# A fused attention and gated MLP layer on one core: a closed head group leaves PSUM in one copy, DMAs move its sums and inverses, GpSimd multiplies and adds the residual, and VectorE's share of the softmax comes in batches of eight

## The chip, the core and the metric

The kernel runs on one core of a Trainium2 chip. The core has five engines with an instruction stream each: TensorE (PE, matmuls; PEld are its weight loads), VectorE (DVE), ScalarE (ACT), GpSimd (POOL) and SyncE (SP), which here only issues DMAs. SBUF is the core's working memory with 128 partitions; PSUM holds the results of matmuls in eight banks of 128 x 512 float32. The metric is the device time of one execution in microseconds (us).

## The reference

The input x is 2048 rows of 512 numbers in bfloat16. All of it is one layer:

```python
xn = _layernorm(x, axis=-1)
q = (xn @ wq) as 32 heads of 16;  k = xn @ wk;  v = xn @ wv      # one key/value head for all
p = softmax(einsum("bhqd,bkd->bhqk", q, k) * 16 ** -0.5)
s = einsum("bhqk,bkd->bhqd", p, v) as (2048, 512) @ wo
g = silu(silu(xn @ w1) @ w2)                                     # 512 -> 1792 -> 512
return x + s * g
```

There is no maximum subtracted and no mask. The 32 heads' scores of 2048 x 2048 (134 million exponentials) are most of the work outside TensorE.

## The kernel before, in words

**Tiles.** Queries are cut into four chunks of 512 (NC). Per chunk there are four "oi" of eight heads each, 16 in all, and each oi is closed in two head groups g = 2*oi + e of four heads. A group has 64 score tiles (SLOTS), each one bank: four 64x32-tile matmuls of `s_half` (L898) fill it with the scores of two heads against 64 keys (128 partitions) for 512 queries. In all there are 2,048 such tiles.

**Two ways to the exponential.** Either ACT takes the exponential of one or two neighbouring banks (`act_step`, L1605) into `pa_sb`; two value matmuls of `do_pv` (L1238) then add the tile to the group's output bank. Or DVE makes a first pass (`pass_d`, L974): it scales and offsets the score into a 16-bit integer whose bits are a bfloat16 near the exponential, in `db_sb`. Four tiles make a batch. POOL then adds three different constants to the whole batch (`split`, L1160, an `int64_add` on words of four numbers) into `ds_sb`, and the sum of the four versions, weighted through four copies of v, approximates the exponential. Such a tile takes eight value matmuls. A version of the shift on DVE (L1156) exists too, but is open only when many shifts wait or in the last group.

**Closing a group.** The value matmuls also carry a column of weights, so that row 16 of each block of 32 in the output bank holds the softmax's sum. When a group is complete, `make_norm` (L1247 to L1274) lets DVE transpose the bank in blocks of 32x32 in place (L1255), take the reciprocal of the sums (L1258), multiply into `otr_sb` (L1260), after which the bank is free, and for each pair of groups transpose back into `on_sb` (L1270). When the four oi of a chunk are in `on_sb`, a "w" job multiplies with wo (`mk_w`); `final` (L764) lets DVE multiply the result with the gate (L766) and add x (L769) into `ob_sb`, and SP stores it (L761). Loads of x for that sum are L777.

**Other work.** LayerNorm and its transposes stand in the first 60 us; "q", "h" and "z" jobs (L665) are the products with wq, w1 and w2, with a tanh on ACT (L713) and a product on DVE (L714) per result.

**Order.** A planner written in Python places every instruction when the kernel is built: it keeps a clock for each engine, charges each task a written duration (T_P 600 ns for a DVE pass, T_P64 for a shift, T_SH for a shift on DVE), and for each engine that is free picks the ready task of lowest priority number. A transfer is charged 60 ns on SP and is visible at issue + 1.4 us + size/(250 bytes per ns) + 0.6 us, the sizes one after the other. The order on each engine is then fixed; semaphore waits keep it right whatever the real durations. `s_step` decides for each free bank whether its tile goes to ACT or DVE by the backlogs of the two; `pick_d` opens a batch for DVE only while a group has at least MARGIN tiles left (MARGIN_END in the last group). Each engine runs its instructions in that order, so an instruction that waits holds all behind it. Tasks with `ports=2` on DVE and POOL are never placed side by side: each waits for the other's last one.

Of the kernel before, what the change touches and what calls it, by code (L numbers as in the profile page):

```python
# [15 lines left out]
P = 128  # L16
# [3 lines left out]
W1_AT, SKIP = 5, 1500.0  # L20
T_ISSUE, T_SWDGE = 450.0, 1000.0
J_BASE, J_END, MIXJ = 0.073, 1.084, 3
# [4 lines left out]
T_P, T_SH, T_TR, T_AF = 600.0, 600.0, 630.0, 63.5  # L27
T_P64, DV_MIN, T_LIB = 1015.0, 40, 300.0
HOLD_PO = 374.374
# [3 lines left out]
Q_URG = 0.308  # L33
J_SLIP = 1.308
NEXT_OB, OB_SLACK = 6, 192.595
NORM_PRIO, T_DIV = 0, 264.0
A_OPEN = 5
T_MS, V_AT = 500.0, 7
# [10 lines left out]
LINE, FETCH, FED, LOOK = 256, 3684.358, 58, 68  # L49
# [3 lines left out]
NPA, NDB, NDS, NTM = 21, 5, 8, 4  # L53
MARGIN, MARGIN_END = 19, 20
WIDE, PAIR_WAIT, GRP_WAIT = 14, 47.267, 237.034
Q_LEAD = 4.233
A_HIGH, D_HIGH, SLACK = 1582.599, 1518.392, 43.301
LEAD, CROWD, FRAG, DB_LOW = 468.141, 0.617, 2.417, 1
RUN, HOLD, PRESS = 6, 1411.229, 18
ROOM = 5  # L60
START_Z, START_H, AHEAD, NEAR = 8, 9, 1.03, 17
CLOSING, URGENT, END_DV = 2, 4.336, 55
STARVED = 511.14
JLATE, JEVAC = 1.311, 1
# [250 lines left out]
def bass_recurrent_scan__grouped_kv_mqa__dense_activation_silu__prompt_kernel(  # L315
# [29 lines left out]
    with ExitStack() as es:  # L345
# [3 lines left out]
        xn_sb = sb("xn_sb", [P, 4, D], BF16)  # L349
# [14 lines left out]
        db_sb = sb("db_sb", [P, NDB, 4 * NQ], U16)  # L364
        ds_sb = sb("ds_sb", [P, NDS, 4 * NQ], U16)
        f_sb = sb("f_sb", [P, 2, NQ], FP32)
        rcp_sb = sb("rcp_sb", [P, 2, NQ // 32], FP32)
        otr_sb = sb("otr_sb", [P, 2, NQ], BF16)
# [5 lines left out]
        ob_sb = sb("ob_sb", [P, 4, D], BF16)  # L374
# [12 lines left out]
        zer_sb = ob_sb[:, 3, :]  # L387
# [3 lines left out]
        XB = NDS - 4  # L391

        def x_tile(t):
            return ds_sb[:, XB + t // 4, (t % 4) * NQ:(t % 4 + 1) * NQ].bitcast(BF16)

# [17 lines left out]
        def xkey(t):  # L413
            return ("Ds", XB + t // 4, t % 4)

        def ds_keys(s):
            return [("Ds", s, h) for h in range(4)]
# [6 lines left out]
        for j in range(1, 4):  # L424
            dma(SP, "x", ds_sb[:, XB + j, :].bitcast(BF16).rearrange("p (t d) -> p t d", d=D),
                xv[:, 4 * j:4 * j + 4, :], 512, ds_keys(XB + j), prio=1)
# [15 lines left out]
        pl.add(Task(DV, 550.0, lambda v: v.memset(zer_sb, 0.0), (), [("ob", 3)], 0))  # L442
# [27 lines left out]
        for e in (1, 0):  # L470
# [16 lines left out]
        m1 = pl.add(Task(AC, 700.0, lambda a: a.activation(f_sb[:, 0, :], x_tile(1), ACT.Copy, scale=1.0 / D,  # L487
                                                          accum_out=mv_sb[:, 1, 0:1]),
                         [xkey(1)], [("F", 0), ("me", 1)], 0, gate=lambda: "scr2" in pl.lastw))
        m2 = pl.add(Task(AC, 210.0, lambda a: a.activation(scr_sb[:, 2:3], mv_sb[:, 1, 0:1], ACT.Copy, scale=-ISD),  # L490
                         [("me", 1)], ["nb"], 0, [m1]))
        pl.add(Task(AC, 700.0, lambda a: a.activation(f_sb[:, 0, :], x_tile(1), ACT.Square, scale=ISD, bias=scr_sb[:, 2:3],
                                                      accum_out=mv_sb[:, 1, 1:2]),
                    [xkey(1), "nb", ("me", 1)], [("F", 0), ("mv", 1)], 0, [m2]))
# [13 lines left out]
        for n in first:  # L508
# [18 lines left out]
            for i in tiles:  # L527
                xn_task[i] = pl.add(Task(DV, 323.0, lambda v, i=i: v.tensor_scalar(  # L528
                    xn_sb[:, i % 4, :], x_tile(i), mv_sb[:, i, 0:1], rstd_sb[:, i:i + 1],
                    op0=ALU.subtract, op1=ALU.mult),  # L530
                    [xkey(i), ("rs", a), ("mv", i)], [("xn", i % 4)], 1 + g, [t], ports=2,
                    gate=lambda i=i: i < 4 or i - 4 in t_done))
# [25 lines left out]
        def mk_T(tiles, bk=None):  # L558
            n, t0 = len(tiles), tiles[0]

            def rnd(b):
                def emit(pe, b=b):
                    dst = bank(b).bitcast(BF16).rearrange("p (t d) -> p t d", d=D)
                    h = None
                    for k, t in enumerate(tiles):
                        for dc in range(NDC):
                            h = pe.transpose(dst[:, k, dc * P:(dc + 1) * P], xn_sb[:, t % 4, dc * P:(dc + 1) * P], ident[:, :])
# [179 lines left out]
        def scaled(tt, b, r=None):  # L747
            k = tt % 2
            if r in EVR:
                ev = pl.add(Task(AC, 490.0, lambda a: a.activation(xn_sb[:, r, :], bank(b), ACT.Copy, scale=0.25),  # L750
                                 [("ps", b)], [("xn", r)], 0))
                fin_task[tt] = Task(DV, 333.0, lambda v: v.tensor_tensor(fin_sb[:, k, :], xn_sb[:, r, :], tmp_sb[:, tt % NTM, :], ALU.mult),
# [7 lines left out]
        def store(tt, t2):  # L760
            return pl.add(Task(SP, 60.0, lambda e: e.dma_start(of.rearrange("(t p) d -> p t d", p=P)[:, tt, :], ob_sb[:, tt % 4, :]),  # L761
                               [("ob", tt % 4)], [("out", tt)], 0, [t2], dma=128 * 1024, on_place=outs.append))

        def final(tt, b):  # L764
            k = tt % 2
            t1 = Task(DV, T_P, lambda v: v.scalar_tensor_tensor(  # L766
                out=bank(b), in0=bank(b), scalar=0.25, in1=tmp_sb[:, tt % NTM, :], op0=ALU.mult, op1=ALU.mult),
                [("ps", b), ("tmp", tt % NTM)], [("ps", b)], 0, [tmp_task[tt]])
            t2 = Task(DV, T_P, lambda v: v.tensor_tensor(ob_sb[:, tt % 4, :], bank(b), xr_sb[:, tt % 4, :], ALU.add),  # L769
                      [("ps", b), ("xr", tt % 4)], [("ob", tt % 4)], 0, [t1, xr_task[tt], out_task.get(tt - 4)])  # L770
# [5 lines left out]
        def add_xr(tt):  # L776
            xr_task[tt] = pl.add(Task(SP, 60.0, lambda e: e.dma_start(xr_sb[:, tt % 4, :], xv[:, tt, :]),  # L777
                                      (), [("xr", tt % 4)], 2, [fin_task[tt - 4]] if tt >= 4 else [], dma=128 * 1024))
# [3 lines left out]
        def mk_w(tt, pace):  # L782
            c, r = divmod(tt, 4)

            def consume(jb, op):
                t1, t2 = final(tt, jb.bank)
                if tt + 4 < NT:
                    add_xr(tt + 4)
                return [t1, t2]
# [151 lines left out]
        def pick_d(t):  # L941
            if st["assigned"] < 8 or any(k not in evac_kt or evac_kt[k].op is None for k in range(NKT)):
                return None
            for bt in batches:
                for k in range(4):
                    if k not in bt.slots and slot_time(bt.g, k % 2) <= t + 20:
                        return bt, k
            if any(len(bt.slots) < 4 for bt in batches):
                return None
            g = st["gD"]  # L950
            while g < NG and (nleft[g] < (MARGIN if g < NG - 1 else MARGIN_END) or min(len(left[g, i]) for i in range(2)) < 2):
# [7 lines left out]
            for k in range(2):  # L959
                if slot_time(g, k) <= t + 20:  # L960
                    bt = Job()
                    bt.g, bt.slots, bt.b, bt.P, bt.nsh, bt.left = g, {}, free[0], {}, 0, 4 * K
# [76 lines left out]
        def start_d(t, b, d):  # L1039
            bt, k = d  # L1040
            g, i = bt.g, k % 2
            if not bt.slots:
                batches.append(bt)
                db_busy[bt.b] = 1
                resv[g, 0], resv[g, 1] = 2, 2
# [63 lines left out]
        def make_shifts():  # L1109
            for bt in list(batches):  # L1110
                if len(bt.slots) < 4:
                    continue
                while bt.nsh < K - 1:
# [4 lines left out]
                    ds_busy[s] = 4  # L1118
# [594 lines left out]
```

## Time and profile before

| What | Value |
|---|---|
| time, median of 3 runs (lowest to highest) | 680.1 us (676.65 to 683.86) |
| time of the profiled execution | 674.7 us |
| its span, first to last instruction | 672.9 us |
| granted TensorE clock, mean | 1.000 |
| busy: PE / ACT / DVE / POOL | 660.8 / 653.9 / 632.6 / 612.1 us |
| score tiles through ACT / through DVE and POOL | 1,256 / 792 |
| HBM read, written | 8.95 MB, 2.10 MB |

A line of a group reads: source line, engine, operation, tile written <- tile read, shapes, count | busy us, mean ns of one | idle time of the engine just ahead of them and who ended it. Busy time counts a moment once even where two instructions of an engine overlap, so it is less than mean times count. A line of a wait reads: engine and line that waited <- engine and line that ended the wait: us in total, times, longest.

### The profile page before, as it was taken

To read this page: it belongs to the slowest core of one execution; us is meant where nothing else is said; L and a number is where in the kernel's file an instruction comes from. 1 tells how busy PE (TensorE), PEld (TensorE's weight loads), DVE (VectorE), ACT (ScalarE), POOL (GpSimd) and SP (SyncE) were. 2 spreads that over 40 slices of the span, in tenths; PEclk is the share of its full clock that TensorE was granted. 3 is DMA by queue.
4 is the path that set the end of the run, shared out by engine and by line. 5 is a ranking of instruction groups with operands and counts; after the bars stand their busy time and mean duration, and the time that the engine had idled before them with its cause. 6 is when DMAs were issued, how large, how long until landed. Compare 5 with 4: busy or idle time off the path is not lost.

```text
span 672.9 us, 47414 instructions
## 1 busy us (share of the span) xinstructions
PE 660.8 (98%) x22086; PEld 373.0 (55%) x22086; DVE 632.6 (94%) x1158; ACT 653.9 (97%) x1172; POOL 612.1 (91%) x610
## 2 busy tenths in 40 slices
PE   8999999999999999999999999999999999999996
PEld 4446656565555655555555656656656555556551
DVE  8989999999999999999999999999999999999932
ACT  6899999999999999999999999999999999999995
POOL 4049899999999999999999999999999999999990
PEclk9999999999999999999999999999999999999999
DMA  6412200000000000000000000000000001000000
GB/s 174 138 50 82 68 4 5 4 5 4 5 4 14 27 21 21 4 5 4 6 5 4 20 20 20 19 5 5 5 4 5 5 20 35 21 4 5 4 5 33
DMA packets 11782, 14.99 MB, mean 22 GB/s; under 512 B 1857, under 2 KB 10817, under 8 KB 11585
## 3 DMA queue, kind: packets, MB, share of 16 engines
q1 hardware_dynamic: 10976, 10.78, 5.4%
q8 instruction: 172, 2.82, 1.7%
q0 software_dynamic: 320, 0.92, 0.5%
q10 hardware_dynamic: 288, 0.26, 0.1%
q14 instruction: 26, 0.20, 0.1%
HBM read 8.95 MB, written 2.10 MB: 16 GB/s over the span
## 4 chain that ended last, share of the span: by engine, by line
PE 74%; ACT 20%; DVE 4%; POOL 1%; issue 0%
PE ps L898 31%; PE ps L1238 26%; ACT pa_sb L1605 19%; PE ps L665 16%; DVE stats_sb L499 1%; ACT t_sb L713 1%; DVE xn_sb L528 1%; POOL kt_sb L461 1%; PE ps L1446 0%; DVE kt_sb L611 0%; DVE xnT_sb L578 0%; DVE v_sb L639 0%; POOL v_sb L459 0%; DVE var_sb L522 0%; DVE var_sb L524 0%
## 5 line engine op out<-in xcount | busy, mean ns | idle before, releaser
L1605 ACT ACTIVATE pa_sb<-ps 128x512 bf16<-128x512 f32 (+1 forms) x1081 | 622.8, 759 | 6.9 <-PE ps L898 6.1
L1160 POOL INT64_ADD ds_sb<-db_sb x594 | 602.8, 1044 | 12.8 <-DVE db_sb L974 6.2
L898 PE MATMUL ps<-qt_sb,kt_sb 64*32 64x512 bf16 x8192 | 564.1, 379 | 0.8 <-issue 0.4
L974 DVE TENSOR_SCALAR db_sb<-ps 128x512 uint16<-128x512 f32 x792 | 493.2, 680 | 10.8 <-PE ps L898 5.9
L1238 PE MATMUL ps<-ds_sb,v_sb 64*32 64x512 bf16 x4752 | 413.6, 377 | 0.8 <-issue 0.6
L1238 PE MATMUL ps<-pa_sb,v_sb 64*32 64x512 bf16 x2512 | 330.7, 377 | 3.0 <-ACT pa_sb L1605 2.3
L898 PEld LDWEIGHTS ps<-qt_sb,kt_sb 64*32 64x32 bf16 x8192 | 197.6, 90 | 190.0 <-ACT pa_sb L1605 81.9
L1238 PE MATMUL ps<-db_sb,v_sb 64*32 64x512 bf16 x1584 | 191.6, 377 | 0.0
L1238 PEld LDWEIGHTS ps<-ds_sb,v_sb 64*32 64x32 bf16 x4752 | 166.7, 92 | 22.0 <-issue 3.4
L665 PE MATMUL ps<-w_sb,u_sb 64*32 64x512 bf16 x1792 | 140.1, 378 | 0.5 <-issue 0.5
L665 PE MATMUL ps<-xnT_sb,w_sb 64*32 64x512 bf16 x1792 | 136.3, 378 | 0.0
L1238 PEld LDWEIGHTS ps<-pa_sb,v_sb 64*32 64x32 bf16 x2512 | 101.6, 92 | 25.1 <-ACT pa_sb L1605 11.1
L1238 PEld LDWEIGHTS ps<-db_sb,v_sb 64*32 64x32 bf16 x1584 | 59.4, 92 | 5.9 <-issue 1.1
L665 PEld LDWEIGHTS ps<-w_sb,u_sb 64*32 64x32 bf16 x1792 | 48.8, 92 | 12.8 <-issue 2.6
L665 PEld LDWEIGHTS ps<-xnT_sb,w_sb 64*32 64x32 bf16 x1792 | 44.3, 91 | 16.4 <-DVE db_sb L974 2.2
L713 ACT ACTIVATE t_sb<-ps 128x512 bf16<-128x512 f32 x72 | 48.9, 679 | 0.0
L1255 DVE STREAM_TRANSPOSE ps<-ps 128x512 f32<-128x512 f32 (+1 forms) x33 | 23.3, 708 | 17.0 <-PE ps L1238 16.8
L714 DVE SCALAR_TENSOR_TENSOR u_sb<-t_sb,ps 128x512 bf16<-128x512 bf16 x56 | 37.9, 676 | 0.5 <-ACT t_sb L713 0.3
L665 PE MATMUL ps<-xnT_sb,wq_sb 64*32 64x512 bf16 x480 | 37.3, 378 | 0.0
L665 PE MATMUL ps<-wo_sb,on_sb 64*32 64x512 bf16 x384 | 29.6, 378 | 0.0
L1284 POOL DMA_DIRECT2D kt_sb<-kt_sb x4 | 2.8, 700 | 23.8 <-DVE kt_sb L611 14.6
L665 PEld LDWEIGHTS ps<-xnT_sb,wq_sb 64*32 64x32 bf16 x480 | 11.7, 91 | 4.1 <-DVE db_sb L974 0.7
(72 smaller groups left out, 181.8 us busy)
## 6 DMA issues: line engine op xcount, KB each, us to landing
xr_sb<-in_A_x_dram SPq DMA_DIRECT2D x16, 128.0 KB, 2.3
out_dram<-ob_sb SPq DMA_DIRECT2D x16, 128.0 KB, 1.7
w_sb<-in_B_w_dram SPq DMA_DIRECT2D x1, 1792.0 KB, 7.2
ds_sb<-in_A_x_dram SPq DMA_DIRECT2D x3, 512.0 KB, 7.0
w_sb<-in_B_w_dram SPq DMA_DIRECT2D x2, 512.0 KB, 4.3
kt_sb<-kt_sb POOLq DMA_DIRECT2D x4, 224.0 KB, 3.7
w_sb<-in_B_w_dram SPq DMA_DIRECT2D x2, 384.0 KB, 4.3
wq_sb<-in_A_wq_dram SPq DMA_DIRECT2D x1, 512.0 KB, 5.2
```

The lines of the kernel that those rows point to most:

```text
L461: pl.add(Task(PO, 3540.0, lambda g: g.memset(kt_sb[0:DH, 1, :, :], 0.0), [("xn", 3)], [("kt1", c) for c in range(NC)], 3, gate=lambda: all ...
L499: ts_ = pl.add(Task(DV, 593.0, lambda v, t=t: v.bn_stats(stats_sb[:, t, :], x_tile(t)), [xkey(t)], [("st", t)], 1 + j, gate=(lambda j=j: S ...
L528: xn_task[i] = pl.add(Task(DV, 323.0, lambda v, i=i: v.tensor_scalar(xn_sb[:, i % 4, :], x_tile(i), mv_sb[:, i, 0:1], rstd_sb[:, i:i + 1], ...
L665: h = pe.matmul(bank(b)[32 * j:32 * (j + 1), :], lhsT=lhs(k, rows, 32 * j, 32), rhs=rhs(k, rows), start=first, stop=last, tile_position=(r ...
L713: t1 = Task(AC, T_AF + 0.8333 * NQ, lambda a: a.activation(t_sb[:, k, :], bank(b), ACT.Tanh, scale=scale), [("ps", b)], [("t", k)], 0)
L714: t2 = Task(DV, T_P, lambda v: v.scalar_tensor_tensor(out=dst, in0=t_sb[:, k, :], scalar=1.0, in1=bank(b), op0=ALU.add, op1=ALU.mult), [(" ...
L898: h = pe.matmul(bank(b)[32 * j:32 * j + 32, :], lhsT=kt_sb[r0:r0 + 64, g % 2, i, k0:k0 + 32], rhs=qt_sb[r0:r0 + 64, g // 2 % NQR, :], star ...
L974: bt.P[k] = pl.add(Task(DV, T_P, lambda v: v.tensor_scalar(db_sb[:, bt.b, k * NQ:(k + 1) * NQ], bank(b), 128.0 * LOG2E, 128.0 * (SHIFT_BET ...
L1160: whole["po"].append(pl.add(Task(PO, T_P64, lambda g: g.int64_add(ds_sb[:, s, :].bitcast(U64), db_sb[:, bt.b, :].bitcast(U64), words), rea ...
L1238: h = pe.matmul(bank(OB)[q:q + 32, :], lhsT=lhs[rows], rhs=rhs[rows], start=s0, stop=s1, tile_position=(64 * l, q), skip_group_check=True)
L1255: t1 = pl.add(Task(DV, (T_TR - 60.0) / parts + 60.0, lambda v, cols=cols: v.transpose(bank(OB)[:, cols], bank(OB)[:, cols]), [("ps", OB)], ...
L1605: op = pl.place(AC, 0.8333 * NQ * n + T_AF, lambda a: a.activation(pa_sb[:, s * NQ:(s + n) * NQ].rearrange("p (b n) -> p b n", n=NQ), ps3[ ...
```

## The change

For the first 15 of the 16 oi, the groups close in another way (`moved_norm`). DVE copies the output bank to SBUF in float32 (`o_sb` for the even group, `e_sb` for the odd one), and the bank is free. DMAs on SP's queue gather the rows of sums of each group into `den_sb` as 128 x 16 numbers; DVE takes one reciprocal for both groups; two DMAs write the inverses to a scratch tensor in DRAM, one DMA fills `rr_sb` from it with each inverse repeated over the 16 rows of its head, four DMAs move the odd group's results to their partitions in `o_sb`; then POOL multiplies `o_sb` with `rr_sb` into `on_sb`. The last oi closes as before. In `final` for all but the last chunk, DVE writes its product to `fin_sb` and POOL adds x in place in `xr_sb`, which is stored from there; `ob_sb` is gone and other small tiles share memory.

Batches have eight tiles in place of four (BS = 8), so each shift is one `int64_add` over 4,096 numbers per partition; `db_sb` has 3 such buffers (5 of four before), `ds_sb` 4 (8 of four), `pa_sb` 24 tiles (21). The planner's written durations and its thresholds have other values, so the order of the whole program and the share of tiles for each engine are planned anew.

```diff
-T_P, T_SH, T_TR, T_AF = 600.0, 600.0, 630.0, 63.5
-T_P64, DV_MIN, T_LIB = 1015.0, 40, 300.0
+T_P, T_SH, T_TR, T_AF = 600.0, 1130.0, 630.0, 63.5
+T_P64, DV_MIN, T_LIB = 1812.0, 40, 300.0
...
+FIN_PRIO, ON_PRIO = 6.803, 3
+T_DMA, T_GT, T_REC = 3200.0, 1300.0, 252.0
...
-NPA, NDB, NDS, NTM = 21, 5, 8, 4
-MARGIN, MARGIN_END = 19, 20
+BS = 8
+NPA, NDB, NDS, NTM = 24, 3, 4, 4
+MARGIN, MARGIN_END = 26, 27
...
-A_HIGH, D_HIGH, SLACK = 1582.599, 1518.392, 43.301
+A_HIGH, D_HIGH, SLACK = 1370.087, 863.23, 45.072
...
-        db_sb = sb("db_sb", [P, NDB, 4 * NQ], U16)
-        ds_sb = sb("ds_sb", [P, NDS, 4 * NQ], U16)
+        db_sb = sb("db_sb", [P, NDB, BS * NQ], U16)
+        ds_sb = sb("ds_sb", [P, NDS, BS * NQ], U16)
...
-        def final(tt, b):
+        def final(tt, b, po=False):
             k = tt % 2
+            if po:
+                t1 = Task(DV, T_P, lambda v: v.scalar_tensor_tensor(
+                    out=fin_sb[:, k, :], in0=bank(b), scalar=0.25, in1=tmp_sb[:, tt % NTM, :], op0=ALU.mult, op1=ALU.mult),
+                    [("ps", b), ("tmp", tt % NTM)], [("fin", k)], 0, [tmp_task[tt], out_task.get(tt - 2)])
+                t2 = Task(PO, T_GT, lambda g: g.tensor_tensor(xr_sb[:, tt % 4, :], fin_sb[:, k, :], xr_sb[:, tt % 4, :], ALU.add),
+                          [("fin", k), ("xr", tt % 4)], [("xr", tt % 4)], FIN_PRIO, [t1, xr_task[tt]], ports=2)
+                fin_task[tt], out_task[tt] = t1, store(tt, t2)
+                pl.add(t2)
+                return [t1]
...
-                for k in range(4):
+                for k in range(BS):
...
-                    bt.g, bt.slots, bt.b, bt.P, bt.nsh, bt.left = g, {}, free[0], {}, 0, 4 * K
+                    bt.g, bt.slots, bt.b, bt.P, bt.nsh, bt.left = g, {}, free[0], {}, 0, BS * K
...
-                if len(bt.slots) < 4:
+                if len(bt.slots) < BS:
...
+        def shift_dma(name, size, out_, in_, reads, writes, preds, prio=-1):
+            task = pl.add(Task(SP, 60.0, lambda e: e.dma_start(out_, in_), reads, writes, prio, preds, dma=size * 1024))
+            task.ring = name
+            return task
+
+        def moved_norm(g):
+            oi, e = divmod(g, 2)
+            OB, k = ob[g], oi % 2
+            okeys = [("xn", 2 * k), ("xn", 2 * k + 1)]
+            dst, keys = (e_sb[:, :], ["eb"]) if e else (o_sb[:, k, :], okeys)
+            ev = norm[g] = pl.add(Task(DV, T_P, lambda v: v.tensor_copy(dst, bank(OB)), [("ps", OB)], keys, NORM_PRIO,
+                                       on_place=lambda op: pool_free.append(OB)))
+            nb = NQ // 32
+            norm["d", g] = shift_dma("den%d" % e, 300, den_sb[:, e, :], dst[DH:P:32], keys, [("den", e)], [ev])
+            if e == 0:
+                return
+            rec = pl.add(Task(DV, T_REC, lambda v: v.reciprocal(inv_sb[:, :, :], den_sb[:, :, :]), [("den", 0), ("den", 1)], ["inv"], 3,
+                              [norm["d", g - 1], norm["d", g]]))
+            put = [shift_dma("put%d" % q, 32, o_sb[32 * q + DH:32 * q + 2 * DH, k, :], e_sb[32 * q:32 * q + DH, :], ["eb", ("den", 0)] + okeys,
+                             [("moved", k, q)], [ev, norm["d", g - 1]]) for q in range(4)]
+            rows = [shift_dma("row%d" % a, 200, in_dram(a * NQ, [[2 * NQ, 4], [16, 32], [1, 16]]), inv_sb[:, a, :], ["inv"], [("row", a)], [rec])
+                    for a in range(2)]
+            fill = shift_dma("fill", 256, rr_sb[:, :], in_dram(0, [[NQ, 8], [0, DH], [1, NQ]]), [("row", 0), ("row", 1)], ["rr"], rows)
+            cc = oi // NOC - NON // NOC
+            t2_task[oi] = pl.add(Task(PO, T_GT, lambda p: p.tensor_tensor(on_sb[:, oi % NON, :], o_sb[:, k, :], rr_sb[:, :], ALU.mult),
+                                      okeys + ["rr"] + [("moved", k, q) for q in range(4)], [("on", oi % NON)], ON_PRIO, put + [fill], ports=2,
+                                      gate=lambda: cc < 0 or all(tt in w_rounds for tt in range(4 * cc, 4 * cc + 4))))
+
         def make_norm(g):
             oi, e = divmod(g, 2)
+            if oi < NO - 1:
+                return moved_norm(g)
```

## The prediction

> **What bounds the kernel now.** I read the page's first parts, then the busy time in windows, the waits, the costliest groups, and last the transfers.
>
> ```profile
> span 672.9 us, 47414 instructions
> PE 660.8 (98%) x22086; PEld 373.0 (55%) x22086; DVE 632.6 (94%) x1158; ACT 653.9 (97%) x1172; POOL 612.1 (91%) x610
> ```
>
> Four engines stand above 90%, so the average names no bound. The windows do (columns: window; then PE, PEld, DVE, ACT, POOL busy us, with instruction counts; clock; DMA share; GB/s):
>
> ```profile
> 25.00:125.00 100.00, 98.10 (x3172) 57.96 (x3176) 95.61 (x176) 96.81 (x177) 79.19 (x79) 1.00 0.14 38
> 225.00:325.00 100.00, 99.99 (x3492) 54.77 (x3484) 99.07 (x171) 99.90 (x185) 99.00 (x98) 1.00 0.04 13
> 325.00:425.00 100.00, 99.92 (x3476) 56.61 (x3468) 97.36 (x168) 99.90 (x179) 100.00 (x100) 1.00 0.06 15
> 650.00:673.00 23.00, 16.45 (x374) 6.06 (x351) 4.71 (x13) 15.67 (x20) 5.96 (x6) 1.00 0.08 25
> ```
>
> In the middle ACT, DVE and POOL are all full, and the clock is full throughout. PE's 99.9% is overlap of pipelined matmuls. From 125 to 625 us it does 17,338 matmuls, 34.7 a us; where the timeline shows it unhindered (near 343 us), a set of four on each of two lanes follows every 0.216 us, 37.0 a us. So PE runs at 94% of its own pace, and the waits name who holds it: mainly ACT, then DVE.
>
> ```profile
> PEld ps L898 <- ACT pa_sb L1605: 81.9, 336, 0.8
> PEld ps L898 <- DVE db_sb L974: 30.4, 136, 0.5
> POOL ds_sb L1160 <- DVE db_sb L974: 6.2, 4, 3.5
> ```
>
> The bound is therefore the joint throughput of ACT, DVE and POOL, which share the 2,048 score tiles: ACT takes the exponential of a tile (L1605), or DVE makes a first pass (L974) and POOL three shifts per batch of four (L1160). Work taken from one is worth something only if tiles are moved until all three are full again.
>
> ```profile
> L1160 POOL INT64_ADD ds_sb<-db_sb x594 | 602.8, 1044 | 12.8 <-DVE db_sb L974 6.2 <-PE ps L1238 4.8 <-PE ps L898 1.6
> L974 DVE TENSOR_SCALAR db_sb<-ps 128x512 uint16<-128x512 f32 x792 | 493.2, 680 | 10.8 <-PE ps L898 5.9 <-POOL ds_sb L1160 2.0 <-PE ps L1238 1.0
> L1255 DVE STREAM_TRANSPOSE ps<-ps 128x512 f32<-128x512 f32 x31 | 22.5, 725 | 3.4 <-PE ps L1238 3.2
> L1260 DVE TENSOR_TENSOR otr_sb<-ps,rcp_sb 128x256 bf16<-128x256 f32 x31 | 12.7, 411 | 0.1
> L1270 DVE STREAM_TRANSPOSE on_sb<-otr_sb 128x512 bf16<-128x512 bf16 x15 | 10.5, 703 | 0.0
> L769 DVE TENSOR_TENSOR ob_sb<-ps,xr_sb 128x512 bf16<-128x512 f32 x13 | 8.8, 678 | 0.0
> L1258 DVE RECIPROCAL rcp_sb<-ps 128x16 f32<-128x16 f32 x31 | 7.5, 240 | 0.1
> L456 POOL INT64_ADD lib_sb<-lib_sb x1 | 0.2, 230 | 0.1
> ```
>
> The reader is to see busy time and mean apart: instructions of one engine overlap at their ends, so the cost of one is busy over count. ACT: 622.8 over 1,256 tiles (906 single, 175 double) = 0.496 us a tile. DVE pass: 493.2/792 = 0.623. Shift: 602.8/594 = 1.015.
>
> **The change, part by part.** *DVE.* Thirty of 32 groups lose transpose, reciprocal and product: 30 x (0.725+0.240+0.411) = 41.3 us. Fifteen pairs lose the second transpose: 15 x 0.703 = 10.5. Added are 30 copies out of PSUM; the nearest row of that shape is L974, so 0.623 to 0.68, taken 0.65: 19.5. Fifteen reciprocals of 2x16: 16 numbers took 0.240, 8 took 0.189, so 32 are estimated at 0.34: 5.1. Twelve residual adds go: 12 x 0.678 = 8.1. Net -35.3 us. The first product of the output keeps its price with another destination.
>
> *POOL, shifts.* One word costs 0.230, 2,048 16-bit numbers per partition (512 words) 1.015, so the slope is 0.785 per four slots and eight cost 1.80 instead of 2.03. Same tiles: 297 x 1.80 = 534.6, that is -68.2. If the start cost is not shared the saving is nothing; that is the other end. Both points come from this operation, so I take 1.80.
>
> *POOL, new elementwise work:* 15 products and 12 adds of 128x512. No row shows a two-input operation on POOL. Below stands the memset of 128x512 (L459, 0.524), above twice the shift (2.09). The product reads 4 KB per partition, as much as the four-slot shift does in 1.04, so 1.2 is taken: 27 x 1.2 = 32.4 (14 to 56). POOL net: -35.8.
>
> [...]
>
> *The new balance.* Let s tiles move from ACT to DVE and POOL. With each engine's idle time kept, the span by ACT is 672.9 - 0.496s, by DVE 637.6 + 0.623s, by POOL 637.1 + 0.675s (three shifts of 1.80 over eight). ACT and POOL meet at s = 35.8/1.171 = 30.6: 657.7 us; DVE is then at 656.7. With s = 0 nothing is gained: ACT stays at 672.9.
>
> *PE.* A moved tile needs eight value matmuls instead of two: 184 more, 5 us at 37.0. PE's pace becomes 34.7 x 1.0085 x 623/608 = 35.9 a us, 97% of its own. That is cover enough, but thin. The closed bank is freed after one copy, 0.7 us, where around 328.8 to 331.1 us it took 2.3; this helps PE to a bank 30 times, and I set the two against each other at zero (each some 2 us).
>
> *Start and end.* POOL's first shift (43.8 us) waits for eight passes instead of four: 2.5 us of POOL, worth 2.5 x 0.496/1.171 = 1.1. At the end DVE's last pass starts at 643.5 and ACT works on alone until 662; a last batch must now open with 27 tiles left, not 20: up to 7 x 0.496 = 3.5, taken 1.7. Buffers hardly change (20 to 24 and 32 to 32 slots).
>
> *Transfers.* Nine DMAs per pair, 135 in all, on SP's queue, which otherwise stands waiting (L761 waits 468.8 us for DVE). An issue there takes 0.34 to 0.51 us, so 58 us of SP, hidden. Queued behind a store that waits for POOL's add are the next group's transfers. The chain sums -> reciprocal -> DRAM -> fill -> product is needed only by the output product some 25 us later, but DVE's reciprocal and POOL's product stand in in-order streams: behind the one are the passes, behind the other the shifts. The written plan gives the chain 3.2 + 0.25 + 3.6 + 3.05 = 10.1 us. The nearest rows:
>
> ```profile
> xr_sb<-in_A_x_dram SPq DMA_DIRECT2D x16, 128.0 KB, 2.3
> kt_sb<-kt_sb POOLq DMA_DIRECT2D x4, 224.0 KB, 3.7
> wk_sb<-in_A_wk_dram SPq DMA_DIRECT2D x1, 16.0 KB, 3.0
> wv_sb<-in_A_wv_dram SPq DMA_DIRECT2D x1, 16.0 KB, 4.2
> ```
>
> Small pieces land in 3.0, or 4.2 behind another. Chain: 3.0 + 0.34 + 0.4 + 3.0 + 3.0 to 3.7 = 9.7 to 10.4, so at most 0.3 us late, which POOL's shift in progress (half of 1.8) covers. I take nothing; with 4.2 for each leg it is 4.2+0.34+0.4+4.2+4.2 = 13.3, 3.2 us late.
>
> Sum: 672.9 - 15.2 + 1.1 + 1.7 = 660.5 span. The profiled execution took 674.7, 1.8 above its span, so 662.3. The median of the runs, 680.1, is 0.8% above that execution: 662.3 x 680.1/674.7 = 667.6, forecast **667 us**.
>
> **The rivals.** *No change.* POOL's two-input operations cost 2.09: POOL gains 68.2 - 56.4 = 11.8, s = 10, the balance 668 and with start and end 670.8, or 678 on the scale of the runs. PE's pace at 97% of its own with eight banks would do the same: its 6% of lost time may not shrink. For it: 81.9 us of waits on ACT. Against: those waits go when ACT is given fewer tiles. That the plan cannot move tiles in steps of eight ends here too, at 675 to 680.
>
> *Slower: late transfers stall full engines.* Each us by which the chain is later than planned stands on POOL (and its first leg on DVE), 15 times, and delays the shifts that PE is to consume. At 3.2 us: 15 x 3.2 = 48 lost, 667 + 48 = 715; at 2 us 697. It decides from 13/15 = 0.9 us per pair, where the gain is gone. For it: the legs are serial and the 4.2 row. Against: that row was taken while 0.66 of the DMA time was in use, and in the middle it is 0.02 to 0.06. [...]
>
> *More than forecast.* POOL's operations at 0.52 and less idle time on DVE (10 us in the middle): 650 to 658.
>
> **How the numbers follow.** Forecast 0.50 (660 to 673), more 0.12, no change 0.16, slower 0.22. Three runs lie within 1% of each other, so about 1% is what can be told from no change. Faster 0.62, same 0.16, slower 0.22. The range leaves out half of the slower case beyond 2 us of lateness and a little below: 650 to 697.
>
> **What would show it.** Passes L974's successor near 822, shifts near 308 at 1.80 us busy; exponential tiles near 1,226; POOL's two-input operations near 1.2; ACT, DVE and POOL full in the middle. Wrong if POOL or DVE show idle time released by a DMA, if shifts cost over 1.9, or if PE waits stay at 110 us while ACT and DVE are no longer full.

## The result, and the profile after

The changed kernel takes 1010.0 us (median, 1006.9 to 1014.88) against 680.29 for the kernel before: a ratio of 1.484 (95% interval 1.477 to 1.491), so 48% slower where 2% faster was forecast. The profiled execution took 1014.88 us, its span is 1013.0, 340.1 more than the 672.9 of before.

The page of the changed kernel, its first part, the granted clock in 40 slices and the shares of the chain that ended last by engine:

```profile
span 1013.0 us, 47350 instructions
PE 720.7 (71%) x22134; PEld 366.2 (36%) x22134; DVE 623.0 (62%) x1096; ACT 663.0 (65%) x1147; POOL 600.0 (59%) x341
PEclk9999897979797797977979869668979797787989
issue 33%; POOL 32%; PE 26%; DVE 4%; ACT 3%; DMA 0%; SPq 0%; POOLq 0%; DVEq 0%
```

The last two of these in the kernel before:

```profile
PEclk9999999999999999999999999999999999999999
PE 74%; ACT 20%; DVE 4%; POOL 1%; issue 0%
```

No engine is near full any more. DVE and POOL do less work than before, ACT 9 us more, and PE's 60 us more come with a lower granted clock (a mean of 0.853, 1.000 before); what has grown is idle time. A third of the chain that ended last is "issue", time in which an engine waited for nothing that the profile shows. The clock, 9 in every slice before, now falls in most of them. The middle, in the same columns as in the prediction:

```profile
225.00:325.00 100.00, 75.43 (x2420) 39.49 (x2408) 67.53 (x111) 71.02 (x124) 62.58 (x35) 0.86 0.06 15
325.00:425.00 100.00, 59.31 (x1772) 29.06 (x1772) 49.74 (x81) 52.41 (x87) 55.92 (x31) 0.81 0.04 12
```

Which engine stops first is told by the waits of the changed kernel (who waited for whom, us in total, times, longest) and by its groups of instructions (busy us, mean ns of one, idle time before them with its releasers):

```profile
ACT pa_sb L1659 <- PE ps L922: 298.7, 94, 13.8
DVE db_sb L998 <- POOL ds_sb L1184: 291.1, 33, 15.6
PEld ps L922 <- DVE db_sb L998: 173.7, 242, 13.8
...
POOL ds_sb L1184 <- issue: 148.4, 25, 6.4
...
POOL on_sb L1295 <- issue: 106.8, 15, 7.7
POOL xr_sb L785 <- issue: 70.8, 10, 7.5
```

```profile
L1184 POOL INT64_ADD ds_sb<-db_sb x298 | 558.2, 1889 | 192.2 <-issue 148.4 <-PE ps L1262 17.3 <-DVE db_sb L998 13.2
L1295 POOL TENSOR_TENSOR on_sb<-o_sb,rr_sb 128x512 bf16<-128x512 f32 x15 | 18.9, 1257 | 106.8 <-issue 106.8
L785 POOL TENSOR_TENSOR xr_sb<-fin_sb,xr_sb 128x512 bf16<-128x512 bf16 x12 | 13.6, 1140 | 70.8 <-issue 70.8
```

ACT waits for PE, PE for DVE, DVE for POOL's shifts, and POOL for nothing that the waits show. The products and adds themselves are short (1.26 and 1.14 us), but 7.1 us of silence stand ahead of one (106.8/15, 70.8/10) and 5.9 us ahead of the shift that follows (148.4/25). Only 10 of the 12 adds have it: two came right behind another product or add. So POOL leaves its shifts and comes back 25 times; each such trip is called an excursion below. 148.4 + 106.8 + 70.8 = 326.0 us, 96% of the 340.1 that the span grew. In the timeline of POOL in the changed kernel (start, us, instructions merged, idle before) it looks like this:

```profile
104.11 37.40 POOL L1184 INT64_ADD ds_sb<-db_sb  x20 [5.79 <-issue]
148.67 1.25 POOL L1295 TENSOR_TENSOR on_sb<-o_sb,rr_sb 128x512 bf16<-128x512 f32 x1 [7.16 <-issue]
156.05 35.53 POOL L1184 INT64_ADD ds_sb<-db_sb  x19 [6.13 <-issue]
```

The list of POOL's instructions in the built program shows what stands there. Before, an instruction without operands came once, ahead of the first `int64_add`. Now one stands wherever the kind changes between `int64_add` and `tensor_tensor` (rows 13, 15 and 17). There are 51 in the changed program, two for each excursion and the first:

```
12 L1184 ISA ds_sb<-db_sb 128x2048 x19
13 L1295 ISA
14 L1295 TensorTensor on_sb<-o_sb,rr_sb 128x512
15 L1184 ISA
16 L1184 ISA ds_sb<-db_sb 128x2048 x20
17 L1295 ISA
18 L1295 TensorTensor on_sb<-o_sb,rr_sb 128x512
```

The trace has it too, under the name MODIFY_POOL_CONFIG, in the views of a single source line (POOLq is POOL's sequencer; times, ns at least, in the middle and at most, first and last start in us). Three lines of the changed kernel, and the one of the kernel before:

```profile
L1295 POOLq MODIFY_POOL_CONFIG  x30: 1/8/16, 89.9 to 969.9; - x30
L785 POOLq MODIFY_POOL_CONFIG  x20: 1/1/33, 289.9 to 892.5; - x20
L1184 POOLq MODIFY_POOL_CONFIG  x50: 1/1/1, 98.5 to 978.3; - x50
L456 POOLq MODIFY_POOL_CONFIG  x2: 11/11/11, 0.9 to 0.9; - x2
```

There are two at each change. They take some nanoseconds; the silence lies behind them, 7.1 us up to the product or add and 5.7 of the 5.9 us up to the shift (in the middle of 25 each).

One such stop in windows of 2 us (columns as above), around the add at 297.03:

```profile
294.00:296.00 2.00, 2.00 (x82) 1.13 (x72) 1.75 (x3) 2.00 (x5) 0.00 (x0) 1.00 0.03 8
296.00:298.00 2.00, 0.68 (x28) 0.11 (x8) 0.00 (x0) 2.00 (x5) 0.97 (x1) 1.00 0.00 0
298.00:300.00 2.00, 0.00 (x0) 0.00 (x0) 0.00 (x0) 0.18 (x1) 0.17 (x1) 0.97 0.21 68
300.00:302.00 2.00, 0.00 (x0) 0.00 (x0) 0.00 (x0) 0.00 (x0) 0.00 (x0) 0.50 0.30 71
...
310.00:312.00 2.00, 2.00 (x48) 0.83 (x40) 1.22 (x2) 0.63 (x2) 2.00 (x2) 0.50 0.03 8
312.00:314.00 2.00, 2.00 (x56) 0.86 (x44) 1.38 (x2) 1.26 (x3) 1.56 (x1) 0.62 0.00 0
```

POOL falls silent near 290; the three buffers of passes cover some 6 us, then DVE, PE and ACT stop within 3 us of each other. About 3.2 us after PE stopped (at 296.7) the clock falls to 0.50, and it is back only some 5 us after PE has resumed (at 308.7): 48 matmuls in 2 us from 310, 82 in 2 us from 294. Over the 25 stops of PE in this trace the fall came 2.3 to 5.3 us after the stop (3.7 in the middle), and the clock was back 2.6 to 10.0 us after PE had resumed (4.5).

### The profile page after: what moved, and what is told of

Same layout as the page of the kernel before. It is cut to its first block, busy times and chain, and to the rows that moved or that the text cites. A ratio compares the mean times of both kernels' runs of the same rounds, so it can differ in the third digit from the quotient of the medians.

```text
span 1013.0 us, 47350 instructions
## 1 busy us (share of the span) xinstructions
PE 720.7 (71%) x22134; PEld 366.2 (36%) x22134; DVE 623.0 (62%) x1096; ACT 663.0 (65%) x1147; POOL 600.0 (59%) x341
## 4 chain that ended last, share of the span: by engine, by line
issue 33%; POOL 32%; PE 26%; DVE 4%; ACT 3%; DMA 0%; SPq 0%; POOLq 0%; DVEq 0%
POOL ds_sb L1184 28%; PE ps L922 11%; PE ps L1262 9%; PE ps L680 5%; ACT pa_sb L1659 3%; POOL on_sb L1295 2%; DVE db_sb L998 1%; POOL xr_sb L785 1%; DVE stats_sb L514 1%; DVE o_sb L543 0%; DMA o_sb<-e_sb 0%; POOL kt_sb L476 0%; PE ps L1500 0%; SPq L1272 0%; DVE kt_sb L626 0%
## 5 line engine op out<-in xcount | busy, mean ns | idle before, releaser
L998 DVE TENSOR_SCALAR db_sb<-ps 128x512 uint16<-128x512 f32 x800 | 504.0, 684 | 353.7 <-POOL ds_sb L1184 291.1
L922 PE MATMUL ps<-qt_sb,kt_sb 64*32 64x512 bf16 x8192 | 605.8, 402 | 109.1 <-DVE db_sb L998 107.1
L1184 POOL INT64_ADD ds_sb<-db_sb x298 | 558.2, 1889 | 192.2 <-issue 148.4
L1262 PE MATMUL ps<-ds_sb,v_sb 64*32 64x512 bf16 x4800 | 396.9, 406 | 72.4 <-POOL ds_sb L1184 70.7
L1262 PE MATMUL ps<-pa_sb,v_sb 64*32 64x512 bf16 x2496 | 264.5, 394 | 31.0 <-POOL ds_sb L1184 29.8
L1262 PE MATMUL ps<-db_sb,v_sb 64*32 64x512 bf16 x1600 | 167.8, 398 | 46.7 <-POOL ds_sb L1184 46.7
L1262 PEld LDWEIGHTS ps<-ds_sb,v_sb 64*32 64x32 bf16 x4800 | 141.3, 97 | 113.8 <-POOL ds_sb L1184 75.7
L1262 PEld LDWEIGHTS ps<-pa_sb,v_sb 64*32 64x32 bf16 x2496 | 81.1, 95 | 57.0 <-POOL ds_sb L1184 33.7
L1295 POOL TENSOR_TENSOR on_sb<-o_sb,rr_sb 128x512 bf16<-128x512 f32 x15 | 18.9, 1257 | 106.8 <-issue 106.8
L785 POOL TENSOR_TENSOR xr_sb<-fin_sb,xr_sb 128x512 bf16<-128x512 bf16 x12 | 13.6, 1140 | 70.8 <-issue 70.8
```

The source lines that it names most:

```text
L785: t2 = Task(PO, T_GT, lambda g: g.tensor_tensor(xr_sb[:, tt % 4, :], fin_sb[:, k, :], xr_sb[:, tt % 4, :], ALU.add), [("fin", k), ("xr", t ...
L922: h = pe.matmul(bank(b)[32 * j:32 * j + 32, :], lhsT=kt_sb[r0:r0 + 64, g % 2, i, k0:k0 + 32], rhs=qt_sb[r0:r0 + 64, g // 2 % NQR, :], star ...
L998: bt.P[k] = pl.add(Task(DV, T_P, lambda v: v.tensor_scalar(db_sb[:, bt.b, k * NQ:(k + 1) * NQ], bank(b), 128.0 * LOG2E, 128.0 * (SHIFT_BET ...
L1184: whole["po"].append(pl.add(Task(PO, T_P64, lambda g: g.int64_add(ds_sb[:, s, :].bitcast(U64), db_sb[:, bt.b, :].bitcast(U64), words), rea ...
L1262: h = pe.matmul(bank(OB)[q:q + 32, :], lhsT=lhs[rows], rhs=rhs[rows], start=s0, stop=s1, tile_position=(64 * l, q), skip_group_check=True)
L1295: t2_task[oi] = pl.add(Task(PO, T_GT, lambda p: p.tensor_tensor(on_sb[:, oi % NON, :], o_sb[:, k, :], rr_sb[:, :], ALU.mult), okeys + ["rr ...
```

## The experiments

The theories, by the letters that the expectations use. S: each change of kind on POOL, to a two-input operation and back, costs its two stops, whatever stands between. L, the slower rival of the prediction: late transfers stall POOL and DVE. B: with batches of eight and few buffers POOL waits for its neighbours, which takes the gain of the longer shift. M: the added transfers disturb the other streams. Ratios are to the kernel before on the same chip.

### One kind of instruction on POOL

The kernel called e1 below: the 27 products and adds become an `int64_add` of 128 words per partition.

```diff
-  ... lambda g: g.tensor_tensor(xr_sb[:, tt % 4, :], fin_sb[:, k, :], xr_sb[:, tt % 4, :], ALU.add)
+  ... lambda g: g.int64_add(xr_sb[:, tt % 4, :].bitcast(U64), fin_sb[:, k, :].bitcast(U64), 0)
-  ... lambda p: p.tensor_tensor(on_sb[:, oi % NON, :], o_sb[:, k, :], rr_sb[:, :], ALU.mult)
+  ... lambda p: p.int64_add(on_sb[:, oi % NON, :].bitcast(U64), xnT_sb[:, 0, 0:NQ].bitcast(U64), 0)
```

> The changed program with the same order on every engine, the same waits and all its transfers; only the 27 two-input operations of POOL (15 products, 12 adds) are int64_add of 128 words on other operands in their place, so the softmax is not normalised and x is not added. Theory S (POOL pays about 7.1 us to change from int64_add to a two-input operation and 5.9 us to change back, by the idle rows of the changed profile: 106.8/15, 70.8/10 and 148.4/25 us): about 1010 - 340 = 670 us, 660 to 680, clock back near 1.0, no idle time of POOL without a releaser. Theory L (the chain of transfers is late and holds POOL and DVE): unchanged, 990 to 1010 us, since every wait is still there.

Measured 680.0 us (677.55 to 681.27), ratio 1.0045 (1.0025 to 1.0065). Order, waits and all transfers are those of the changed kernel, the built program has the instruction without operands once, and 330 us are gone. Page and POOL's timeline of this kernel:

```profile
span 679.4 us, 47250 instructions
PE 661.1 (97%) x22134; PEld 358.6 (53%) x22134; DVE 617.8 (91%) x1096; ACT 653.0 (96%) x1147; POOL 577.9 (85%) x341
```

```profile
127.86 0.40 POOL L1295 INT64_ADD on_sb<-xnT_sb  x1
128.24 35.60 POOL L1184 INT64_ADD ds_sb<-db_sb  x19
```

The shift follows its stand-in at once. L falls: the transfers are there and nothing is late. But the rest of the forecast does not appear either: with the stops gone this is 0.45% slower than before, not 1.9% faster, although the stand-ins take 10.8 us of POOL (6.0 + 4.8) where the prediction charged 32.4. The later experiments are about that.

### The stop counted, in the changed kernel and in the kernel before

The residual add goes back to DVE in the changed kernel, which leaves 15 excursions of 25:

```diff
-                tasks = final(tt, jb.bank, True)
+                tasks = final(tt, jb.bank)
```

> The changed program with the residual add back on DVE: 15 two-input operations on POOL are left of 27. Theory S: 340/27 = 12.6 us each, so about 1010 - 12 x 12.6 = 859 us (840 to 880) and 15 long idle stretches ahead of the products, 15 behind. Theory L: the adds do not hang on the chain of transfers, so about 1000 us (980 to 1010).

Measured 877.81 us (one run). Ten excursions fewer are worth 1013.0 - 875.9 = 137.1 us of span, 13.7 each; the 859 of the expectation had counted every add as one, 12 of them. What is left of the stops:

```profile
POOL on_sb L1295 <- issue: 108.8, 15, 7.7
POOL ds_sb L1184 <- issue: 88.4, 15, 6.0
```

Next the kernel before, with one tiny addition on POOL (128 x 16 numbers, which nothing uses) at each of 15 closings, and then with four back to back:

```diff
+  def twos(p):
+      for n in range(1):      # range(4) in the second
+          r = p.tensor_tensor(two_sb[:, n, :], two_sb[:, 4, :], two_sb[:, 4, :], ALU.add)
+      return r
+  pl.add(Task(PO, 300.0, twos, ["two"], ["two4"], 3, [norm["m", g, h]]))
   (the added tile two_sb is cleared once at the start)
```

> The kernel before with one added POOL operation at each of 15 closings: a tensor_tensor add of 128x16 float32 on a tile nobody else uses, 0.3 us by its size. None of the transfers is there. Theory S: 680 + 15 x 12.6 = 869 us (850 to 890). Theory L: 680 to 685 us.

> As the kernel before with one added operation at 15 closings, but with four of them back to back at each, in the same order otherwise. Theory S, the price is for each change of kind: as with one, plus 45 x 0.2 to 0.3 us, 10 to 15 us more. Rival: the price is for each two-input operation on POOL: 680 + 60 x 12.6, about 1436 us. Theory L: 690 to 700 us.

Measured 870.49 and 877.78 us (one run each), before 676.47. Fifteen operations of 0.20 us cost 194.0 us, 12.9 each; 45 more of them cost 7.3, no more than two runs of one kernel differ by (676.65 and 683.86 of the kernel before); their busy time grows from 3.0 to 10.7 us. The waits of the kernel with 15, then the timeline and two windows of the one with 60:

```profile
POOL two_sb L1274 <- issue: 106.6, 15, 7.6
POOL ds_sb L1162 <- issue: 88.3, 15, 6.2
```

```profile
131.86 0.71 POOL L1274 TENSOR_TENSOR two_sb<-two_sb 128x16 f32<-128x16 f32 x4 [7.11 <-issue]
138.56 39.59 POOL L1162 INT64_ADD ds_sb<-db_sb  x39 [5.99 <-issue]
```

```profile
124.80:131.80 7.00, 3.27 (x108) 1.49 (x92) 2.72 (x5) 3.64 (x6) 0.00 (x0) 1.00 0.01 2
132.60:138.50 5.90, 0.00 (x0) 0.00 (x0) 0.00 (x0) 0.00 (x0) 0.00 (x0) 0.50 0.00 0
```

106.6 + 88.3 = 194.9 us is the whole loss. The price is one of the excursion, not of the operation, its size, the batches of eight or the new close. In the second stop shown no engine does anything and no transfer is on record, so nothing hides it. In the changed kernel the gap behind the MODIFY_POOL_CONFIG is 5.7 us on the way back and 7.1 on the way in, and it is paid at every change but the program's first. What POOL does in the gap is not shown; the runs show where it stands and what it costs. The transfers of instructions on record do not grow with the changes: 198 packets in the kernel before, 199 and 200 in the two with 15 excursions, 197 in the changed one with 25.

### All the work, none of it of another kind

Product and residual add on DVE, everything computed, the planner's thresholds chosen anew by the plan's own length (as in all kernels below that are not said to keep their order; 13 to 26 constants of the planner differ from the changed kernel's, in the one with batches of four 33, and with them the order):

```diff
-            t2_task[oi] = pl.add(Task(PO, T_GT, lambda p: p.tensor_tensor(on_sb[:, oi % NON, :], ...
+            t2_task[oi] = pl.add(Task(DV, T_P, lambda p: p.tensor_tensor(on_sb[:, oi % NON, :], ...
-                tasks = final(tt, jb.bank, True)
+                tasks = final(tt, jb.bank)
```

> The changed kernel with products and residual adds on DVE (15 more operations of 128x512 there, float32 from SBUF, and 12 adds), everything computed; thresholds chosen anew. No change of kind is left on POOL. Theory S: 675 to 688 us, clock 1.0; by the order of my sum DVE keeps 18 of the 35 us that were to leave it. If two SBUF inputs on DVE hold POOL up, POOL's shifts beside them grow past 1.9 us and it is over 690.

Measured 680.66 us, ratio 1.002 (0.9991 to 1.0048). So S holds with nothing left out: a product costs DVE 0.686 us, and 15 of them and 12 adds cost some 18 us of DVE where the stops alone cost POOL 326.

```profile
L1295 DVE TENSOR_TENSOR on_sb<-o_sb,rr_sb 128x512 bf16<-128x512 f32 x15 | 10.3, 686 | 1.3 <-POOL ds_sb L1184 1.1
```

### What became of the longer shift

Batches of eight alone: the close and the add as before the change.

```diff
-                tasks = final(tt, jb.bank, True)
+                tasks = final(tt, jb.bank)
-            if oi < NO - 1:
-                return moved_norm(g)
```

> Batches of eight alone: groups close as before on DVE, the residual add is on DVE, no transfers, no two-input operation on POOL; thresholds of the planner chosen anew for it. Theory B: POOL again waits 20 us or more for value matmuls and the time is 678 to 686 us, not better than before, since DVE and ACT get nothing. Theory M: POOL's waits are as before (under 8 us) and the time 670 to 677 us.

Measured 676.24 us, ratio 0.996 (0.9929 to 0.999). Then, on top of it, a fifth buffer of shifts, and separately the measured price of a shift in the plan:

```diff
-T_P64, DV_MIN, T_LIB = 1812.0, 40, 300.0
+T_P64, DV_MIN, T_LIB = 1872.0, 40, 300.0     # in both
-NPA, NDB, NDS, NTM = 24, 3, 4, 4
+NPA, NDB, NDS, NTM = 18, 3, 5, 4             # in the first
```

> Batches of eight alone, with five shift buffers of eight tiles in place of four (40 slots, paid with 18 ACT tiles in place of 24), the real 1.87 us charged for a shift, thresholds chosen anew. Theory B (a buffer of eight comes free only as a whole, so POOL stands waiting for value matmuls): POOL's waits for value matmuls fall from 31 us to under 15, and the time from 676 to 668 to 673 us. If those waits stay or the time stays at 674 to 680 us with them gone, the buffers are not what holds it.

> Batches of eight alone, four shift buffers, but the planner charges the shift at 1.872 us, as the runs show, in place of 1.812 (298 x 0.06 = 18 us over the run); thresholds chosen anew. If the too short charge is what puts the other engines out of step: 669 to 674 us and POOL's waits under 40 us in all. If not: 675 to 679 us, waits near 60 as before.

Measured 676.07 us, ratio 0.9986 (0.9964 to 1.0008), and 672.1 us, ratio 0.9919 (0.9888 to 0.9949). POOL's shifts, of batches of eight alone and, in the second fence, with the fifth buffer:

```profile
L1184 POOL INT64_ADD ds_sb<-db_sb x297 | 556.9, 1898 | 61.0 <-PE ps L1262 31.2 <-DVE db_sb L998 17.0 <-PE ps L922 12.5
```

```profile
L1181 POOL INT64_ADD ds_sb<-db_sb x297 | 556.5, 1899 | 51.4 <-DVE db_sb L995 43.7 <-PE ps L1259 5.7 <-PE ps L919 1.6
```

B saw a true thing and drew the wrong conclusion: POOL does wait for the value matmuls to free a buffer (31.2 us, 5.7 with a fifth), but without that wait it waits for DVE's passes instead, and the time is the same. Against the kernel with the same price and four buffers, the one with five is even 0.7% slower; it has six ACT tiles less and another order, and what costs it that is not shown. POOL's idle time is surplus. The window from 125 to 625 us of batches of eight alone, and in the second fence of the one with the measured price:

```profile
125.00:625.00 500.00, 497.09 (x17164) 292.37 (x17156) 488.44 (x836) 496.62 (x908) 458.13 (x245) 1.00 0.04 11
```

```profile
125.00:625.00 500.00, 498.23 (x17285) 284.72 (x17277) 490.43 (x839) 497.29 (x911) 460.06 (x247) 1.00 0.04 11
```

DVE and ACT are full (488 to 490 and 497 of 500), POOL has 40 us to spare. The longer shift takes work from the one engine of three that cannot be swapped against ACT alone: each tile moved off ACT costs DVE a pass as well. The expected drop of POOL's waits in the last kernel did not come (54.3 us, 61.0 before); its time did. A last variant of it shows how much of the 0.8% is one lucky order. DVE's pass is planned at 608 ns, and the thresholds are chosen again:

```diff
-T_P, T_SH, T_TR, T_AF = 600.0, 1130.0, 630.0, 63.5
+T_P, T_SH, T_TR, T_AF = 608.0, 1130.0, 630.0, 63.5
```

> Batches of eight alone with the close and the residual add as before, planned with the shift at 1.872 us and the DVE pass at 0.608; thresholds chosen anew. With the shift's price alone it was 0.992. If the durations in the plan are what matters: 0.985 to 0.992. If that was luck of one order: 0.992 to 1.000.

Measured 676.36 us, ratio 0.9958 (0.9934 to 0.9982). Batches of eight by themselves are worth 0.1 to 0.8%, 0.4% in the middle, and the order decides where in that. The one at 672.1 beats both kernels of this case.

### Why the moved close does not pay

It frees DVE, and yet e1 and the kernel with all on DVE are no faster than before. Three suspects. The transfers (M): the nine of each pair cut to 64 bytes, in the kernel with stand-ins on POOL and in its order, so normalisation and residual are left out.

```diff
-  fill = shift_dma("fill", 256, rr_sb[:, :], in_dram(0, [[NQ, 8], [0, DH], [1, NQ]]), ...
+  fill = shift_dma("fill", 256, rr_sb[0:1, 0:16], in_dram(0, [[NQ, 1], [1, 16]]), ...
   (the other eight alike; the reciprocal reads rstd_sb)
```

> As the run with one kind of operation on POOL (680 us), same order and same waits, but each of the nine transfers per pair moves only 64 bytes (the reciprocal then reads another tile): sums, moved rows, inverses and fill are left out of the data. It asks what holds that version at 680 us where my sum had 667. Theory M (the transfers slow the loading of instructions, so that PE waits with no releaser: the PEld rows marked issue grew from about 20 to 30 us): 669 to 674 us, these rows back near 20. Theory B (batches of eight: a buffer comes free only when all eight tiles are consumed; POOL waited 28.6 us for value matmuls, 4.8 before): unchanged, 678 to 682 us.

Measured 678.68 us, ratio 0.9995 (0.996 to 1.003), where the full transfers had 1.0045 (1.0025 to 1.0065). M is wrong in its mechanism: PE's waits without releaser did not fall (29.2 us summed over its rows, 27.6 with the full transfers). The intervals just touch, so the bytes may cost some 0.5%, about what e1 lost against before, or next to nothing. They are not why the freed DVE gains nothing: without them it is still no faster than the kernel before.

The batches: four in place of eight, with the moved close and the stand-ins.

```diff
-BS = 8
-NPA, NDB, NDS, NTM = 24, 3, 4, 4
+BS = 4
+NPA, NDB, NDS, NTM = 21, 5, 8, 4
-T_DMA, T_GT, T_REC = 3200.0, 1300.0, 252.0
+T_DMA, T_GT, T_REC = 3200.0, 400.0, 252.0
   (T_SH and T_P64 as in the kernel before: 600.0 and 1015.0)
```

> The moved close with batches of four (eight shift buffers of four, five first-pass buffers of four), POOL's two-input operations again replaced by int64_add of 128 words, so normalisation and residual add are left out; thresholds chosen anew. Theory B: POOL's waits for value matmuls are back under 10 us. POOL has no relief then (594 shifts of 1.015), so DVE's 35 us buy little by my sum: 672 to 680 us.

Measured 685.3 us, ratio 1.0106 (1.0061 to 1.0151). POOL's groups of this kernel:

```profile
L1184 POOL INT64_ADD ds_sb<-db_sb x570 | 579.6, 1042 | 18.8 <-DVE db_sb L998 13.6 <-PE ps L922 3.1 <-PE ps L1262 1.3
L1295 POOL INT64_ADD on_sb<-xnT_sb x15 | 6.0, 399 | 4.1 <-DMA rr_sb<-inv_dram 3.9
```

The waits went as expected (1.3 us for the value matmuls), the time did not: it got longer. So the batches of eight are not it either. The second line measures the lateness of the chain of transfers directly: 3.9 us over all 15 pairs. Side by side, the moved close costs 1.1% with batches of four and, with batches of eight, some 0.8% (1.002 to 1.0045 against 0.996, 0.9958 and 0.9919), so as far as kernels with orders of their own can tell, it is the close that does not pay.

The planned durations: the kernel with all on DVE, with the measured prices of shift, pass and reciprocal in the plan.

```diff
-T_P, T_SH, T_TR, T_AF = 600.0, 1130.0, 630.0, 63.5
-T_P64, DV_MIN, T_LIB = 1812.0, 40, 300.0
+T_P, T_SH, T_TR, T_AF = 608.0, 1130.0, 630.0, 63.5
+T_P64, DV_MIN, T_LIB = 1872.0, 40, 300.0
...
-T_DMA, T_GT, T_REC = 3200.0, 1300.0, 252.0
+T_DMA, T_GT, T_REC = 3200.0, 1300.0, 330.0
```

> The changed kernel with products and residual adds on DVE, everything computed, as once before (1.002 of the kernel before), but planned with durations as the runs show them: shift 1.872 us, DVE pass 0.608, reciprocal 0.33; thresholds chosen anew. If the planned durations are what kept the moved close from paying: 0.985 to 0.995 of the kernel before, and the waits of DVE for PE and of PE for DVE (21.9 and 54 us) fall by a third. If not: 0.998 to 1.006, waits as they were.

Measured 681.35 us, ratio 1.0038 (1.001 to 1.0066). Not it, although PE's waits for DVE fell as asked, from 54.0 to 31.9 us; those for ACT grew from 47.6 to 58.9, those of DVE for PE from 21.9 to 25.3. What the kernels with the moved close share is seen in the same window, of e1, and in the second fence of the kernel before:

```profile
125.00:625.00 500.00, 491.23 (x16972) 268.76 (x16968) 464.22 (x765) 491.21 (x869) 460.70 (x267) 1.00 0.08 21
```

```profile
125.00:625.00 500.00, 499.23 (x17274) 284.05 (x17268) 489.97 (x838) 498.50 (x904) 494.45 (x489) 1.00 0.04 11
```

DVE is freed (464 of 500, 26 less than before), but the plan hardly gives it more passes for that (800 over the whole run, 792 before; 792 and 784 in the two with the work on DVE); and PE, which should go faster, does 33.9 matmuls a us against 34.5. The waits between these two, of e1:

```profile
PEld ps L922 <- ACT pa_sb L1659: 59.0, 236, 1.5
PEld ps L922 <- DVE db_sb L998: 46.1, 189, 0.8
...
DVE db_sb L998 <- PE ps L922: 18.6, 41, 1.8
```

PE waits longer for DVE than before (46.1 us, 30.4) while DVE waits longer for PE (18.6, 5.9): each stands for the other, with both below full. In no kernel of this study did PE do more than 34.6 a us over this window, of the 37.0 that it reaches unhindered near 343 us of the kernel before. The chains that ended last point the same way. By engine, in e1, in the kernel with all on DVE, and in the fastest one (672.1 us):

```profile
PE 83%; ACT 6%; DVE 5%; POOL 3%; issue 1%
PE 93%; DVE 5%; issue 1%; ACT 0%
PE 94%; DVE 4%; DMA 1%; issue 1%; SPq 0%; ACT 0%; DVEq 0%
```

PE had 74% of it before, and has 77% with the moved close and batches of four. With batches of eight the chain runs almost wholly over PE, and DVE's share of it is 4 to 6%. That fits the rival "no change", in which eight banks do not let PE lose less. It is not shown: no run had another number of banks, and the number of transfers (135) was not varied either. Why a freed DVE brings nothing stays open.

## Why the prediction was wrong, point by point

**The step that failed** is "POOL, new elementwise work", 27 x 1.2 = 32.4 us. Its durations came out right in the sum, 18.9 + 13.6 = 32.5 us, in part by luck: the 1.2 was drawn from the bytes of a product (1.257 measured), and the add, with half of them, takes 1.140. What it left out is the change of kind. No row of the profile before holds one, since POOL did only `int64_add`, memsets and DMA issues there; the bounds, 0.52 to 2.09 us, were drawn around the instruction, and what stands between two instructions was given none. Measured, the step costs 32.5 + 326.0 = 358.5 us. The row L456, quoted for its 0.230 us, stands just behind the one such instruction of the program before, but with 0.1 us of idle time ahead of it: the stop does not show there, and why the first one is free is not known. So no row could have given the price; a second bound, on what may stand ahead of an operation that the stream has never held, was missing.

**The slower rival** had the right side and the wrong mechanism. The chain of transfers, taken at 0 us late, was late by 0.3 us per pair where it could be measured (3.9/15); e1 keeps all 135 transfers at 680.0. SP's new issues are longer than taken (0.54 to 0.64 us, not 0.34 to 0.51) and hidden, as predicted.

**The shift of eight** was mis-sized: 558.9/298 = 1.876 us in e1, not 1.80, and 297 of them save 45 us of POOL, not 68.2. The line through 0.230 and 1.015 was too flat.

**The balance** failed next. It put 30.6 tiles from ACT to the other two; the plan moved 8 (800 passes, 792 before, where 822 were named; 864 + 2 x 192 = 1,248 exponential tiles, not 1,226). With s = 8 the prediction's own line for ACT gives 672.9 - 4.0 + 1.1 + 1.7 = 671.7 of span, 678.9 on the scale of the runs. The freed time was there, on DVE and on POOL, and no order used it. Against before this is 0.2% better, and e1 measured 0.45% worse: the last 0.6% are what stays open above, and the bytes of the transfers may be a part of them. PE's pace of 34.7 was read a little high: five windows added count the matmuls on their borders twice, and the whole stretch has 17,274, 34.5 a us.

**Right, and without weight:** copies out of PSUM, 0.65 taken, 20.4/30 = 0.68 measured; reciprocals, 0.34 and 0.343:

```profile
L1281 DVE COPY o_sb<-ps 128x512 f32<-128x512 f32 x15 | 10.2, 683 | 0.2
L1287 DVE RECIPROCAL inv_sb<-den_sb 128x32 f32<-128x32 f32 x15 | 5.1, 343 | 0.0
```

The start cost more than taken: POOL's first shift is at 47.4 us, 3.5 later, not 2.5. **The tests named for a wrong prediction** did not ask for the stops. Two stayed silent: in the middle no idle time of POOL or DVE is released by a DMA, and a shift costs 1.87 us, not over 1.9. The third, PE's waits near 110 us while ACT and DVE are no longer full, is met in e1 (59.0 + 46.1 us, DVE at 464 of 500): it saw what is left once the stops are gone. The sign of the stops was idle time released by nothing.

## What to carry to other kernels

When an operation is new to an engine's stream, ask two prices: its own duration and that of changing to it and back. Between these two kinds on GpSimd count the changes, not the instructions: keep one kind there, or put all operations of the other kind together, since four in a row at each closing cost hardly more than one (877.78 us against 870.49). And time freed on one of several engines that share work counts only as far as the order moves work onto it: on a set that is full together, predict from the tiles that the plan moves, not from the balance it could reach.

## What the runs showed of the hardware that was not expected

- A change from `int64_add` to `tensor_tensor` on POOL takes 7.1 us and the change back 5.9, at every change but the first, with no wait on record: two MODIFY_POOL_CONFIG of some nanoseconds stand at its start, and then nothing. Memsets and DMA issues among `int64_add` show none: in the kernel before, the memset behind the first `int64_add` has 2.15 us of idle time ahead of it and the shift behind the last DMA issue 3.52, both ended by DVE, and neither line shows a MODIFY_POOL_CONFIG.
- A stop of one engine for 13 us became one of PE for 7 to 13 us, 10.5 in the middle: at 290 us the batches in flight covered only some 6. On top, PE's clock was at 0.50 for its first 2.6 to 10.0 us afterwards, 4.5 in the middle (mean 0.853 over the span, 1.0 in e1).
- The two-input operations themselves are 1.7 to 1.8 times as long on POOL as on DVE: 1.14 us for the residual add of 128x512, where DVE took 0.678 (with one input from PSUM), and 1.257 for the product, where DVE took 0.686.
